# Graph tensor product: the second part's first sorting pass starts ten units into the main phase instead of beside the first sorted segment

## The chip, the cores and the metric

The kernel runs on one core of a Trainium2 chip. The core has five engines that run their own instruction streams in order: PE (TensorE: matrix products; its weight loads, PEld, overlap them), DVE (VectorE), ACT (ScalarE), POOL (GpSimd; here it issues the indirect DMAs, one row of DRAM for each of 128 partitions) and SP (SyncE; here it issues the plain DMAs). The metric is the device time of one execution in microseconds (us), the median of three runs.

## The reference, cut to what matters

```python
N, deg, C, L, DE = 10000, 64, 64, 1, 4          # E = 640000 edges, M = 4
R   = silu(edge_feat @ w_rad)                    # (E, 64)
xs  = x[src]                                     # (E, 64, 4): one 1 KB row of x for each edge
tp  = einsum('eci,ef,ifo->eco', xs, Y, cg)       # (E, 64, 4)
msg = R[:, :, None] * tp
agg = segment_sum(msg.reshape(E, 256), dst, N)   # random, unsorted destinations
out = einsum('ncm,cd->ndm', agg.reshape(N, 64, 4), w_mix)
```

Sources and destinations of the edges are drawn at random. So each edge needs a gathered row of x, and its message has to be added into a row that nothing orders.

## The kernel before

The kernel sorts the edges by destination and then sums them with matrix products. The 640,000 edges are 5,000 tiles of 128, cut into three parts (30%, 35.5% and 34.5%). Each part goes through two sorting passes:

- `pass1(k)` reads part k and writes each edge's record (9 words: source and destination packed, four Y, four features) into one of 18 groups of 576 nodes (tensor `grp`).
- `pass2` takes the groups of a part one after the other (a **segment** is one group of one part, 54 in all; the last group, which is the smallest, comes first) and writes its records into buckets of 32 nodes (tensor `bkt`). A segment's finished buckets are loaded back as `pay` (L818).

Both passes consist of a **front**, which counts digits and builds tables (`digits`, `tables`: a chain of many small operations that goes back and forth between DVE, PE and ACT, L333 to L510), and a **route**, which moves a chunk of tiles (12 in pass 1, 11 in pass 2) at a time: `spread` (L571, L574: the records spread by slot into `X`, on DVE), `rows` (L590 on DVE, L596 and L597 on ACT: one-hot matrices `oh`), `move` (L604, and in pass 2 L606 with the row carried over from the chunk before: matrix products, PE), `evict` (L611, ACT) and `store` (L615: indirect DMA from POOL). In shapes, a pass 1 chunk is 128x1512 in L574, a pass 2 chunk 128x1485 (945 for a short last one). Pass 1 works in batches of chunks, each with its own front; the first batch of a part in this phase has 14 chunks, the next ones some 12 to 13. A part of 148 chunks (the second) is counted by the planner as 878.7 steps.

`messages()` consumes the buckets. A **unit** is one bucket of one part: 313 units of 5 tiles for the first part, 313 of 6 tiles for the second and the third, 939 in all. For each unit `index` (L863 to L867, DVE) takes the sources out of `pay`, `gather` (L911, POOL) issues one indirect DMA for each tile into `xg` (7 units of buffers), PE and ACT compute the radial weights (L929 to L945), DVE multiplies them in (`products`, L963, once for each unit, which makes it the clock of this phase in the trace), and PE adds up the bucket (`sums`, L976). The buffer `xg` of a unit comes free when its `sums` are done. `messages` yields four times for each unit; such a step is called a quarter here, numbered v. A unit's index is issued 8 units, its gather 5 units ahead, so quarters 0 to 31 issue only preparations, the first unit's multiplication L963 stands at v = 30, and unit n's at about v = 30 + 4n.

The program has three stretches. First, `pass1(0)` alone. Then the **opening**: `pass2` sorts the first segment, and the loop at L1077 takes one step of `pass1(1)` after each of its steps. Then the **main phase**: a loop over v that interleaves three streams by hand, since PE, DVE and ACT are scheduled manually there (the order of the code is the order on these engines; POOL and SP are placed by the framework). For each v it first takes steps of the next part's pass 1, then steps of `pass2` for the segment that is needed next, then one quarter of `messages`. Pass 1 of the second part must end before quarter 1128, and its pace is linear:

```python
first, at, end, n = later[0]
while done < n * (v + 1 - at) / (end - at) or due:
    said = next(first, "end")
    done += said or 1
```

In the kernel before, `at` is 0, `done` starts with what the opening took (68 steps) and another 11 steps are taken in quarters 0 to 9 because `due` is set while pass 1 holds a shared PSUM bank. These 79 steps are ahead of the line that starts at 0 with a slope of 878.7/1128 = 0.779 steps a quarter, so none is taken from quarter 10 to quarter 100. The second segment has to be sorted by quarter 4 (`ends[0]`), so its sort is taken as one burst at the beginning of the main phase; from then on segments are spread over the quarters. While pass 1 holds the bank, the burst gets "held" and waits; it comes in quarter 9.

Of the kernel before, what the change touches and what calls it, by code (L numbers as in the profile page):

```python
# [68 lines left out]
def run(gen):  # L69
    for _ in gen:  # L70
        pass


class Kernel:
# [983 lines left out]
    def groups(self):  # L1058

        self.pay = {}  # L1060
        sort, main, segs, NG = self.pass2(), self.messages(), self.segs, self.NG

        ends, u = [], 0
        for k, g in segs:
            u += self.nb(g) * len(SPLIT[k][1])
            ends.append(4 * max(u - LI - 3, ends[-1] // 4 + 1 if ends else 1))

        for k in range(1, len(SPLIT)):
            ends[k * NG - 1] -= 22

        later, at = [], 0
        for k in range(1, len(SPLIT)):
            end = max(ends[k * NG - 2] - 8, at + 1)
            n = self.chunks(k)
            later.append((self.pass1(k, self.p1.NC), at, end, HEAVY * n + 20 * (n / (self.p1.NC - 2) + 2)))
            at = end
        done = 0.0  # L1077
        while segs[0] not in self.pay:
            next(sort)
            if later:  # L1080
                said = next(later[0][0])
                done += 0.0 if said == "held" else said or 1
        acc = 0.0
        i = start = 0
        for v in range(4 * u):

            if later:
                first, at, end, n = later[0]
                due = "grp" in (self.held, self.pos)
                while done < n * (v + 1 - at) / (end - at) or due:  # L1090
                    due = False
                    said = next(first, "end")
                    if said == "end":
                        later.pop(0)
                        done, self.sorted = 0.0, self.sorted + 1
                    if said in ("held", "end"):
                        break
                    done += said or 1
            if i + 1 < len(segs):
                acc += self.pass2_steps(*segs[i + 1]) / (ends[i] - start)  # L1100
                due = "bkt" in (self.held, self.pos)
                while (acc > 0.0 or v >= ends[i] or due) and segs[i + 1] not in self.pay:
                    due = False
                    said = next(sort)
                    if said == "held":
                        break
                    acc -= said or 1
                if v >= ends[i] and segs[i + 1] in self.pay:
                    i, start, acc = i + 1, ends[i], 0.0
            next(main)  # L1110
        assert not later
        run(main)
        run(sort)
# [176 lines left out]
```

## Time and profile before

| | |
|---|---|
| median of three runs | 8613.98 us (8609.68 to 8615.34) |
| the profiled execution | 8636.13 us, span 8634.0 us |
| granted TensorE clock, mean | 0.904 |
| instructions | 150016 |
| pass 1 of the first part ends | at about 527 us |
| first load of the opening (L762) | 532.6 us |
| first gather (L911) | 633.6 us |
| first unit's multiplication (L963) | 716.1 us |

The page gives busy times by engine; a table of busy times in chosen stretches shows which engine is full where, a list of instructions in order of time shows single waits ("[0.98 <-ACT pre L945]": the engine was idle for 0.98 us before this one, until ACT's L945 released it), and a group row gives count, busy time, mean duration in ns and the idle time before the group. Times count from the start of the span. The work that the change moves all lies between 532 us and the multiplication of unit 258 (2775.6 us).

### The profile page before, as it was taken

How to read it: one execution, taken by the hardware profiler on the slowest of the kernel's cores; microseconds unless marked ns; L12 is line 12 of the kernel's file. 1: busy time of each engine (PE TensorE's matmuls, PEld its weight loads, DVE VectorE, ACT ScalarE, POOL GpSimd, SP SyncE). 2: the span in 40 equal slices, each digit the busy share in tenths (PEclk: the TensorE clock that was granted, in tenths of full speed). 3: DMA queues.
4: the chain of work that ended last, by engine and by line, in shares of the span. 5: the costliest groups of instructions: out<-in, count | busy, mean ns of one | idle time of the engine just before them, and what ended most of it. 6: DMA issues, size and time to landing. Idle time of an engine off the chain costs nothing. (4 is left out here: it accounts for less than half of the span.)

```text
span 8634.0 us, 150016 instructions
## 1 busy us (share of the span) xinstructions
PE 6890.9 (80%) x52148; PEld 6320.9 (73%) x52148; DVE 6821.4 (79%) x13093; ACT 4619.2 (54%) x13164; POOL 6034.7 (70%) x6308
## 2 busy tenths in 40 slices
PE   7977888888888778888788888876888878788875
PEld 5867777777777677777777777766777767777764
DVE  7988888888888788898888988876766767676743
ACT  6867666666666465555555655534443434343421
POOL 1226777767777767777777777777777777777775
PEclk9989999999999889999999999988988989898987
DMA  9313444344434434444444444444444444444442
GB/s 160 109 58 101 121 118 119 108 115 117 122 111 116 122 104 134 134 132 138 133 132 137 133 133 133 130 139 130 128 125 125 126 124 124 122 129 124 125 123 83
DMA packets 696294, 1056.68 MB, mean 122 GB/s; under 512 B 252018, under 2 KB 500226, under 8 KB 695536
## 3 DMA queue, kind: packets, MB, share of 16 engines
q0 software_dynamic: 286560, 746.71, 30.3%
q1 hardware_dynamic: 406384, 292.76, 12.6%
q8 instruction: 412, 6.75, 0.3%
q10 hardware_dynamic: 2592, 7.63, 0.3%
q14 instruction: 346, 2.83, 0.1%
HBM read 856.08 MB, written 207.12 MB: 123 GB/s over the span
## 5 line engine op out<-in xcount | busy, mean ns | idle before, releaser
L911 POOL DMA_INDIRECT xg<-in_x_dram,sidx x5321 | 5062.5, 951 | 1713.8 <-issue 1399.6
L604 PE MATMUL pr<-X,oh 128*128 128x126 f32 (+1 forms) x21112 | 2803.6, 291 | 490.1 <-ACT rt L611 321.7
L604 PEld LDWEIGHTS pr<-X,oh 128*128 128x128 f32 x21112 | 2664.2, 202 | 584.8 <-ACT rt L611 377.8
L976 PE MATMUL G<-S,xg 128*128 128x128 f32 x21284 | 2863.7, 296 | 139.0 <-DVE Gp L1005 98.5
L976 PEld LDWEIGHTS G<-S,xg 128*128 128x128 f32 x21284 | 2715.3, 209 | 178.3 <-DVE Gp L1005 120.0
L963 DVE TENSOR_TENSOR xg<-xg,pre 128x1536 f32<-128x1536 f32 (+1 forms) x939 | 1557.8, 1659 | 888.5 <-DMA xg<-in_x_dram,sidx 648.5
L596 ACT ACTIVATE sq<-i,rowf 128x128 f32<-128x128 f32 x6403 | 1969.4, 393 | 21.7 <-DVE rowf L561 21.2
L574 DVE TENSOR_TENSOR X<-dv,Wt 128x1512 f32<-128x1512 f32 (+4 forms) x958 | 1588.4, 1658 | 221.7 <-PE pr L604 171.1
L945 ACT ACTIVATE pre<-pre 128x384 f32<-128x384 f32 (+1 forms) x939 | 431.6, 460 | 1477.3 <-PE pre L942 1125.0
L597 ACT ACTIVATE oh<-sq,ones 128x1024 f32<-128x1024 f32 (+4 forms) x958 | 1017.6, 1062 | 27.4 <-ACT sq L596 0.3
L956 DVE TENSOR_TENSOR S<-dv,pay 128x768 f32<-128x768 f32 (+1 forms) x939 | 857.4, 913 | 60.4 <-PE G L976 15.6
L615 POOL DMA_INDIRECT grp<-rt,idx x417 | 415.3, 996 | 592.5 <-ACT rt L611 256.1
L615 POOL DMA_INDIRECT bkt<-rt,idx x541 | 542.1, 1002 | 219.8 <-issue 129.2
L590 DVE TENSOR_TENSOR oh<-dv,rowf 128x512 f32<-128x512 f32 (+2 forms) x904 | 684.0, 761 | 0.5
L929 PE MATMUL pre<-identb,e 128*108 128x128 bf16 x1878 | 275.2, 230 | 418.4 <-DVE xg L963 410.9
L929 PEld LDWEIGHTS <-e 128*108 128x108 bf16 x1878 | 218.3, 133 | 496.9 <-issue 411.0
L934 ACT ACTIVATE sT<-pre 108x256 bf16<-108x256 f32 x939 | 352.3, 375 | 429.4 <-PE pre L929 428.2
L1024 PE MATMUL po<-wf,Gs 128*128 128x256 f32 (+2 forms) x1392 | 392.7, 445 | 163.6 <-DVE Gs L1005 163.3
L1024 PEld LDWEIGHTS po<-wf,Gs 128*128 128x128 f32 (+2 forms) x1392 | 284.2, 210 | 254.8 <-DVE Gs L1005 179.4
L611 ACT ACTIVATE rt<-pr 128x135 f32<-128x135 f32 (+1 forms) x958 | 258.6, 273 | 259.5 <-DMA bkt<-rt,idx 188.4
L941 PE MATMUL pre<-wr,sT 108*128 108x192 bf16 x939 | 239.7, 255 | 182.4 <-ACT sT L934 180.6
L544 ACT ACTIVATE pc<-pp 128x432 f32<-128x432 f32 (+3 forms) x506 | 243.3, 481 | 251.0 <-DVE pos L553 149.5
(240 smaller groups left out, 5347.5 us busy)
## 6 DMA issues: line engine op xcount, KB each, us to landing
xg<-in_x_dram,sidx POOLq DMA_INDIRECT x5321
sums<-Gp SPq DMA_DIRECT2D x626, 128.0 KB
old<-sums SPq DMA_DIRECT2D x626, 128.0 KB
bkt<-z SPq DMA_DIRECT2D x24, 994.5 KB
pay<-bkt SPq DMA_DIRECT2D x34, 486.0 KB
ys<-in_Y_dram SPq DMA_DIRECT2D x104, 96.0 KB
es<-in_edge_feat_dram SPq DMA_DIRECT2D x104, 96.0 KB
out_dram<-ot SPq DMA_DIRECT2D x69, 128.0 KB
```

Source lines behind the costliest of these rows:

```text
L574: nc.vector.tensor_tensor(X[:, :m, :].rearrange("p t (s w) -> p t s w", w=W), msk.unsqueeze(3).to_broadcast([P, m, ps.r, W]), QD[c // Q][1 ...
L590: nc.vector.tensor_tensor(oh[:, :v, :], self.v128.unsqueeze(1).to_broadcast([P, v, P]), row[:, o:o + v].unsqueeze(2).to_broadcast([P, v, P ...
L596: nc.scalar.activation(sq[:, u, :], self.i128, AF.Square, bias=to, scale=-1.0)
L597: nc.scalar.activation(oh[:, v:v + len(at), :], sq[:, :len(at), :], AF.Relu, bias=self.ones[:, 0:1], scale=-2.0)
L604: nc.tensor.matmul(pr[:, :ps.rw], oh[:, u, :], X[:, u, :], start=(u == 0), stop=(not on and u == m - 1))
L615: st = nc.gpsimd.indirect_dma_start(out=ps.dst, out_offset=bass.IndirectOffsetOnAxis(ap=idx[:, i:i + 1], axis=0), in_=RT.pop(c), in_offset ...
L911: nc.gpsimd.indirect_dma_start(out=xg[:, t, :], out_offset=None, in_=self.x, in_offset=bass.IndirectOffsetOnAxis(ap=si[:, u:u + 1], axis=0))
L929: nc.tensor.matmul(pre[:KR, 256 + 128 * h:384 + 128 * h], e[:, 36 * t:36 * t + KR], self.identb, start=True, stop=True)
L956: nc.vector.tensor_tensor(S[:, :ut], self.eq[:, :ut].unsqueeze(3).to_broadcast([P, ut, NB, 4]), pb[:, :, 1:5].unsqueeze(2).to_broadcast([P ...
L963: nc.vector.tensor_tensor(V, V, R.unsqueeze(3).to_broadcast([P, ut, 64, 4]), op=OP.mult)
L976: nc.tensor.matmul(G[:, h].rearrange("p n f -> p (n f)"), V[:, t, 32 * h:32 * h + 32, :].rearrange("p c i -> p (c i)"), S[:, t].rearrange( ...
L1024: nc.tensor.matmul(po[:nn, :256], Gs[:, h, f].rearrange("p b n -> p (b n)")[:, :nn], self.wf[:, h, f, :], start=(h + f == 0), stop=(h + f ...
```

## The change

The loop that sorts the first segment no longer takes a step of `pass1(1)` after each step, and the line by which `pass1(1)` is paced in the main phase starts at quarter 40 (ten units) instead of 0, with `done` = 0. Its end, quarter 1128, stays, so the slope is 878.7/1088 = 0.808 steps a quarter.

```diff
-        later, at = [], 0
+        later, at = [], 40
         for k in range(1, len(SPLIT)):
             end = max(ends[k * NG - 2] - 8, at + 1)
...
         done = 0.0
         while segs[0] not in self.pay:
             next(sort)
-            if later:
-                said = next(later[0][0])
-                done += 0.0 if said == "held" else said or 1
```

On DVE, at the beginning of the opening, the rows of the two passes alternated. Before (`dg_6054`, `two` from it and L375 with `onbkt` belong to the first segment's front, `key` and `da` to that of pass 1 of the second part):

```order
933 L772 TENSOR_SCALAR base<-bb 128x18
934 L778 TENSOR_SCALAR dg_6054<-Wt_6050 128x40
935 L779 TENSOR_SCALAR dg_6054<-dg_6054 128x40
936 L666 MEMSET k_238 1x18
937 L333 CAST two<-dg_6054 128x80
938 L690 TENSOR_SCALAR key<-da 128x168
```

and now:

```order
933 L772 TENSOR_SCALAR base<-bb 128x18
934 L778 TENSOR_SCALAR dg_6054<-Wt_6050 128x40
935 L779 TENSOR_SCALAR dg_6054<-dg_6054 128x40
936 L333 CAST two<-dg_6054 128x80
937 L338 TENSOR_TENSOR D_6057<-dv,two 128x720
938 L375 SCALAR_TENSOR_TENSOR sums<-onbkt,colsbkt 64x216
```

From row 933 to the first unit's multiplication, DVE has 425 rows before (the multiplication is row 1358) and 303 now (row 1236). Gone from there are two fronts and nine chunks of pass 1; one more chunk of the third segment now stands ahead.

On POOL, around the first gathers, the stores of pass 1 (`grp`) and pass 2 (`bkt`) and the gathers (`xg`). Before:

```order
20 L615 DMA grp<-rt,idx 165888x126 x126
21 L615 DMA bkt<-rt,idx 229888x135
22 L615 DMA grp<-rt,idx 165888x126 x2
23 L615 DMA bkt<-rt,idx 229888x135 x3
24 L911 DMA xg<-in_x_dram,sidx 128x256 x35
25 L615 DMA bkt<-rt,idx 229888x135 x12
26 L911 DMA xg<-in_x_dram,sidx 128x256 x5
```

and now:

```order
20 L615 DMA grp<-rt,idx 165888x126 x124
21 L615 DMA bkt<-rt,idx 229888x135 x4
22 L911 DMA xg<-in_x_dram,sidx 128x256 x9
23 L615 DMA bkt<-rt,idx 229888x135
24 L911 DMA xg<-in_x_dram,sidx 128x256 x7
25 L615 DMA bkt<-rt,idx 229888x135
26 L911 DMA xg<-in_x_dram,sidx 128x256 x9
27 L615 DMA bkt<-rt,idx 229888x135
28 L911 DMA xg<-in_x_dram,sidx 128x256 x10
29 L615 DMA bkt<-rt,idx 229888x135 x10
```

Four stores of pass 1 that stood ahead of the first gather now stand behind it (128 before, 124 now); the first seven units' 35 gathers stand ahead of most of the second segment's stores in both.

On DVE, just ahead of the fourth unit's multiplication L963, pass 1's first front now begins (rows L666 to L333, and L338 with `D_7490`; `Wt_6443` is the third segment's):

```order
1274 L574 TENSOR_TENSOR X<-dv,Wt_6443 128x1485
1275 L666 MEMSET k_238 1x18
1276 L690 TENSOR_SCALAR key<-da 128x168
1277 L691 TENSOR_TENSOR si<-key,si 128x168
1278 L692 TENSOR_SCALAR da<-da 128x168
1279 L333 CAST two<-da 128x336
1280 L590 TENSOR_TENSOR oh<-dv,rowf 128x512
1281 L953 TENSOR_TENSOR dv<-dv,dlc 128x160
1282 L956 TENSOR_TENSOR S<-dv,pay 128x640
1283 L338 TENSOR_TENSOR D_7490<-dv,two 128x720
1284 L963 TENSOR_TENSOR xg<-xg,pre 128x1280
```

where before (at the fifth unit's multiplication; `Wt_6939` is again the third segment's) no row of pass 1 stood for 17 units:

```order
1407 L902 TENSOR_TENSOR er<-pay,e_7990 128x100
1408 L571 TENSOR_TENSOR dv<-dv,slot 128x165
1409 L574 TENSOR_TENSOR X<-dv,Wt_6939 128x1485
1410 L953 TENSOR_TENSOR dv<-dv,dlc 128x160
1411 L956 TENSOR_TENSOR S<-dv,pay 128x640
1412 L590 TENSOR_TENSOR oh<-dv,rowf 128x512
1413 L963 TENSOR_TENSOR xg<-xg,pre 128x1280
```

Pass 1 of the second part ends at quarter 1072 before and at quarter 1074 now. From the multiplication of unit 258 to the end of the program, DVE's rows are the same ones in the same order.

## The prediction

> **What bounds the kernel now.** I read the table of busy times by stretch first, because the page's shares average over stages with different limits.
>
> ```profile
> core 0: us, PE busy (x) PEld busy (x) DVE busy (x) ACT busy (x) POOL busy (x), PEclk, DMA share, GB/s
> 536.00:716.00 180.00, 115.98 (x723) 98.31 (x724) 140.77 (x428) 105.08 (x305) 51.24 (x54) 0.76 0.18 50
> 716.00:827.00 111.00, 93.85 (x780) 87.24 (x779) 99.39 (x203) 72.84 (x212) 79.34 (x83) 0.98 0.42 120
> 827.00:2776.00 1949.00, 1619.17 (x12771) 1507.19 (x12772) 1673.70 (x3221) 1275.56 (x3716) 1418.79 (x1473) 0.92 0.41 116
> 3500.00:8500.00 5000.00, 3992.57 (x29761) 3662.86 (x29761) 3790.45 (x6853) 2340.53 (x6503) 3791.02 (x3964) 0.90 0.45 129
> ```
>
> From 3500 us to the end POOL makes 3964 indirect DMAs in 5000 us, one in 1.261 us. Next, its rows in order of time, to see what it waits for between two.
>
> ```profile
> 633.64 0.99 POOL L911 DMA_INDIRECT xg<-in_x_dram,sidx  x1 [9.55 <-DVE didx L865]
> 634.93 0.97 POOL L911 DMA_INDIRECT xg<-in_x_dram,sidx  x1 [0.30 <-issue]
> 636.21 0.95 POOL L911 DMA_INDIRECT xg<-in_x_dram,sidx  x1 [0.31 <-issue]
> ```
>
> A busy 0.95 to 0.97 us and 0.30 us of "issue" make about 1.25 us: back to back, POOL can go no faster, so from 3500 us on POOL is full although its busy share there is only 76%. Between 827 and 2776 us it makes 1473, which would need 1473 x 1.261 = 1857 of the 1949 us: 92 us short of full. There something else sets the pace at times. The multiplications L963 against their gathers tell which:
>
> ```profile
> 716.14 1.48 DVE L963 TENSOR_TENSOR xg<-xg,pre 128x1280 f32<-128x1280 f32 x1
> 826.82 1.48 DVE L963 TENSOR_TENSOR xg<-xg,pre 128x1280 f32<-128x1280 f32 x1
> 2775.64 1.49 DVE L963 TENSOR_TENSOR xg<-xg,pre 128x1280 f32<-128x1280 f32 x1 [0.98 <-ACT pre L945]
> 2834.56 1.48 DVE L963 TENSOR_TENSOR xg<-xg,pre 128x1280 f32<-128x1280 f32 x1
> ```
>
> These are units 0, 18, 258 and 270. The POOL rows that end the gathers of 258 and 270:
>
> ```profile
> 2736.14 0.95 POOL L911 DMA_INDIRECT xg<-in_x_dram,sidx  x1 [0.31 <-issue]
> 2827.74 0.94 POOL L911 DMA_INDIRECT xg<-in_x_dram,sidx  x1 [0.30 <-issue]
> ```
>
> Unit 258 is multiplied 38.6 us after its last gather was issued, unit 270 only 5.9 us after. So up to 258 the computing engines are behind and POOL waits for free buffers; then, with pass 1 of the second part over, they catch up with POOL. The waits of 716 to 2776 us agree:
>
> ```profile
> POOL xg L911 <- PE G L976: 48.9, 31, 6.0
> DVE xg L963 <- DMA xg<-in_x_dram,sidx: 13.8, 9, 4.3
> ```
>
> POOL waited 48.9 us for finished sums, DVE only 13.8 us for gathers. DVE is the fullest of the engines: 99.39 of 111 us, then 1673.70 of 1949 (86%, the rest being round trips with PE and ACT). So up to unit 258 time goes by DVE's rows, and what counts is how far unit 258 shifts: behind it DVE's rows are the same before and after.
>
> **The change, part by part.** I priced every row of DVE's order at the busy time that its line adds on the average in this trace. For the 425 rows ahead of the first multiplication that gives 140.8 us, which is the 140.77 of the first stretch; for the 303 rows now it gives 99.2 us, so 41.6 us leave the opening. The largest groups of pass 1 in the opening (536 to 716 us):
>
> ```profile
> L574 DVE TENSOR_TENSOR X<-dv,Wt 128x1512 f32<-128x1512 f32 x9 | 15.6, 1732 | 1.9 <-PE pr L604 1.4
> L590 DVE TENSOR_TENSOR oh<-dv,rowf 128x640 f32<-128x640 f32 x8 | 6.5, 815 | 0.0
> L553 DVE TENSOR_REDUCE pos<-pc 128x24 f32<-128x432 f32 x6 | 3.6, 594 | 0.4 <-ACT pc L544 0.4
> L571 DVE TENSOR_TENSOR dv<-dv,slot 128x168 f32<-128x168 f32 x9 | 3.0, 332 | 0.0
> ```
>
> Those are 28.7 us; two fronts of many small rows and less of the same kind make the rest, and a chunk and some table rows of the third segment, which now stand ahead of the first multiplication, take about 15 us back.
>
> Opening: DVE idled 180 - 140.8 = 39.2 us in it. Part of that was pass 1's doing, because DVE waited for PE behind the other pass's products:
>
> ```profile
> 578.02 1.71 DVE L574 TENSOR_TENSOR X<-dv,Wt 128x1485 f32<-128x1485 f32 x1 [3.67 <-PE pr L604]
> 591.94 1.71 DVE L574 TENSOR_TENSOR X<-dv,Wt 128x1485 f32<-128x1485 f32 x1 [4.02 <-PE pr L604]
> 618.66 0.39 DVE L465 SCALAR_TENSOR_TENSOR to<-sts,pid,gop 128x171 f32<-128x171 f32 x1 [4.00 <-PE gop L462]
> 693.10 0.24 DVE L778 TENSOR_SCALAR dg<-Wt 128x95 int32<-128x95 int32 x1 [5.25 <-DMA Wt<-grp]
> ```
>
> The first three go (11.7 us), the fourth, a load, stays. That bounds the idle time from below at 27; from above at 39, since a table chain that pass 1's rows used to fill is now bare. I take 30, nearer to the low end, because the second segment's chunks alone kept DVE nearly full. First multiplication: 536 + 99.2 + 30 = 665, 51 us earlier (42 to 54). POOL allows it: by the same prices 40.0 us of DVE's rows stand ahead of the first index where 72.4 did, so the first gather comes at about 536 + 40 + 17 = 593 instead of 633.64, and 35 gathers and nine stores (44 x 1.261 = 55) end at 649. Pass 1's loads of Y, features and indices leave SP's queue there and return ten units later; nothing in the opening waits for SP but the segments' own loads.
>
> Units 0 to 18: nothing of pass 1 stood there; now 49 steps do (60.5 quarters by 0.808). DVE's rows grow from 106.6 to 134.7 us. The stretch took 110.7 us for 106.6, so it was DVE alone; scaled alike, 134.7 take 139.9: +29. Bounds: +28 with no waits, and 134.7 / 0.859 - 110.7 = +46 with the waits of the next stretch. PE stays behind DVE: it was busy for 93.85 us of this stretch, and six chunks at 2.81 us (the row is quoted below) and small products add some 20 in 140.
>
> Units 18 to 258: the steeper line (0.808 against 0.779) adds the remaining 30 steps; DVE's rows grow by 13.1 us. At 86% that is +15, at the lowest 0, if they fall into the round trips' gaps. I take +13, since fronts and chunks come in bursts in which DVE has no gaps.
>
> POOL has four more stores behind the first gather, 4 x 1.261 = 5 us; they are covered as long as DVE leads, and the cover holds: POOL waits 48.9 us for sums. From unit 258 on everything is as before, only shifted; POOL, at most seven units ahead, shifts along.
>
> Sum: -51 + 29 + 13 = -9 us. The profiled execution took 8636.13 us, which makes 8627; it lies 22 us above the median of the runs, 8613.98, which makes **8605 us**, 0.1% less. Lowest: -54 + 28 + 0 = -26; highest: -42 + 46 + 15 = +19. About 0.2% (17 us) is what a measurement of this kernel can tell from no change, so this is a forecast of no change: work moves from one stretch where DVE sets the pace to another.
>
> **The rivals.** *POOL is the bound all along* (faster). For it: POOL is within 92 us of full already between 827 and 2776 us, and it starts 40 us earlier. Then moved DVE work would hide behind the gathers, and only the start and four stores count: -40 + 5 = -35, 8579 us. Against it: 38.6 us of backlog at unit 258, and 48.9 us of POOL waiting for sums. It decides if DVE's extra 41 us find gaps; there are 1949 - 1673.7 = 275 us of gaps, but in short round trips.
>
> *The opening runs at half clock* (slower). With fewer products PE may not earn its full clock there.
>
> ```profile
> 532.00:624.00 92.00, 54.98 (x321) 45.61 (x322) 65.69 (x204) 49.64 (x148) 7.68 (x8) 0.67 0.12 32
> 644.00:693.00 49.00, 36.80 (x262) 32.23 (x261) 39.32 (x98) 36.14 (x101) 33.21 (x35) 0.92 0.33 96
> 538.46 0.78 PE L365 MATMUL cnt<-D,sel 128*64 128x198 bf16 x4 [11.57 <-DMA es<-in_edge_feat_dram]
> 652.94 5.32 PE L604 MATMUL pr<-X,oh 128*128 128x135 f32 x22 [2.77 <-DVE oh L590]
> 660.03 2.81 PE L604 MATMUL pr<-X,oh 128*128 128x135 f32 x22 [0.56 <-ACT rt L611]
> 664.68 2.79 PE L604 MATMUL pr<-X,oh 128*128 128x135 f32 x22 [1.60 <-DVE dl L430]
> 662.69 0.39 PE L606 MATMUL pr<-rt,oh 128*128 128x135 f32 x2
> ```
>
> Even with pass 1 the granted clock was 0.67 from 532 to 624 us, and a chunk of pass 2 takes 5.32 us at the low clock instead of 2.81. Each chunk's product with the carried row waits for the eviction of the one before, so at the low clock a chunk would need 5.32 + 2 x 0.39 + about 0.3 = 6.4 us instead of the 4.65 between 660.03 and 664.68: 1.8 us more. Ahead of the first multiplication now stand 4 + 9 + 5 = 18 chunks; if all ran so, the time would be -9 + 18 x 1.8 = +23, 8637 us. It passes +17 from some 15 chunks on. Against it: with pass 2 alone, from 644 to 693 us, the clock was 0.92.
>
> [...]
>
> *The change does not do what it says.* The order rules this out for the opening; that pass 1 ends at quarter 1074 against 1072 rules out a later next part.
>
> **How the numbers follow.** The sum: 0.49, all of it counted within 0.2%. POOL, with the cases in which DVE finds gaps for most of what is moved: 0.25, faster. The clock, or waits in units 0 to 18 at their upper bound: 0.26, slower. The range reaches from the POOL case's near side (8584) to the clock's full price (8637), which leaves out about 2 in 10.
>
> **What would show it.** First gather near 593, first multiplication near 665 (654 to 674), unit 18 near 805, unit 258 near 2767, and from there the same shift to the end. DVE nearly full in units 0 to 18, POOL's waits for sums longer there. Wrong in the first term if the first multiplication is later than 680; wrong in the second if units 0 to 18 take under 125 or over 157 us; wrong altogether if unit 258 shifts otherwise than the end does.

## The result and the profile after

The changed kernel takes 8595.4 us (median of 18 runs, 8588.25 to 8604.24); the kernel before, run beside it, takes 8611.53 us (18 runs, 8601.73 to 8620.35). The ratio is 0.9982, with a 95% interval of 0.9974 to 0.9989: 16 us less, a gain that is real and lies just inside the 0.2% that the prediction called no change. The forecast was 8605.

The profiled execution of the changed kernel took 8589.39 us (span 8587.6). In it the opening begins at 515.4 us instead of 532.6. That difference of 17 us lies ahead of every changed instruction: among the six profiled executions of these kernels on such chips the opening began between 515.4 and 537.8 us, the changed kernel itself at 535.3 in another one. So in what follows, times count from the first load of the opening (L762) of the same execution.

The table of busy times by stretch, changed kernel (columns as in the prediction's first fence; the first four stretches are the opening and units 0 to 18, 18 to 90 and 90 to 258):

```profile
core 0: us, PE busy (x) PEld busy (x) DVE busy (x) ACT busy (x) POOL busy (x), PEclk, DMA share, GB/s
519.00:646.00 127.00, 79.20 (x511) 66.03 (x511) 95.83 (x299) 77.39 (x218) 49.41 (x52) 0.77 0.21 57
646.00:782.00 136.00, 115.27 (x919) 106.68 (x919) 128.96 (x279) 90.28 (x267) 96.12 (x101) 0.94 0.42 121
782.00:1364.00 582.00, 480.67 (x3794) 446.11 (x3793) 505.99 (x1003) 377.26 (x1101) 421.48 (x439) 0.92 0.40 116
1364.00:2730.00 1366.00, 1134.96 (x9019) 1058.61 (x9020) 1183.15 (x2268) 904.96 (x2636) 979.18 (x1018) 0.93 0.40 114
3500.00:8500.00 5000.00, 3978.04 (x29745) 3653.18 (x29743) 3773.85 (x6807) 2327.03 (x6461) 3791.91 (x3965) 0.90 0.45 130
```

The prediction took units 18 to 258 of the kernel before in one piece (827 to 2776 us). Cut at unit 90, the same view of the kernel before reads:

```profile
core 0: us, PE busy (x) PEld busy (x) DVE busy (x) ACT busy (x) POOL busy (x), PEclk, DMA share, GB/s
827.00:1422.00 595.00, 490.42 (x3840) 454.86 (x3841) 505.46 (x981) 383.82 (x1119) 440.04 (x457) 0.91 0.41 117
1422.00:2776.00 1354.00, 1128.75 (x8933) 1052.33 (x8933) 1168.24 (x2242) 891.74 (x2599) 978.76 (x1016) 0.93 0.40 115
```

The reader is to see two things. Units 18 to 90 became 13 us shorter although DVE is as busy there as before (505.99 against 505.46 us); POOL has 18 DMAs less to make there, 439 against 457, and 101 instead of 83 in units 0 to 18. Units 90 to 258 became 12 us longer, with 15 us more of DVE's rows.

The first two gathers, and the multiplications of units 0, 18, 90 and 258 (POOL's and DVE's rows in order of time, changed kernel):

```profile
567.44 0.99 POOL L911 DMA_INDIRECT xg<-in_x_dram,sidx  x1 [10.34 <-DVE didx L865]
568.73 0.97 POOL L911 DMA_INDIRECT xg<-in_x_dram,sidx  x1 [0.30 <-issue]
...
645.49 1.49 DVE L963 TENSOR_TENSOR xg<-xg,pre 128x1280 f32<-128x1280 f32 x1
781.56 1.48 DVE L963 TENSOR_TENSOR xg<-xg,pre 128x1280 f32<-128x1280 f32 x1
1363.44 1.48 DVE L963 TENSOR_TENSOR xg<-xg,pre 128x1280 f32<-128x1280 f32 x1
2729.59 1.48 DVE L963 TENSOR_TENSOR xg<-xg,pre 128x1280 f32<-128x1280 f32 x1
```

From these rows come the stretches (before, unit 90 is multiplied at 1421.93 us); the column f1 is another profiled execution of the changed kernel, on another chip (run f1 below).

| stretch | before | changed | difference | changed, f1 | predicted difference |
|---|---|---|---|---|---|
| opening to first multiplication | 183.5 | 130.1 | -53.4 | 131.5 | -51 |
| units 0 to 18 | 110.7 | 136.1 | +25.4 | 135.1 | +29 |
| units 18 to 90 | 595.1 | 581.9 | -13.2 | 583.2 | |
| units 90 to 258 | 1353.7 | 1366.2 | +12.5 | 1365.8 | |
| units 18 to 258 together | 1948.8 | 1948.1 | -0.7 | 1949.0 | +13 |
| opening to unit 258 | 2243.0 | 2214.2 | -28.8 | 2215.6 | -9 |
| opening to the last multiplication | 8020.0 | 7992.6 | -27.4 | 7998.6 | same shift as 258 |

In the traces the gain up to unit 258 is 27 to 29 us, and 21 to 27 of it reaches the last multiplication; the medians show 16. A trace is a single execution, and where the remaining 5 to 11 us go is not known. So two of the three terms hold and the third, units 18 to 258, is where the forecast was about 14 us too high.

The waits between 646 and 2730 us, the same stretch of work as 716 to 2776 us before (us in total, times, longest):

```profile
POOL xg L911 <- PE G L976: 69.7, 30, 9.7
DVE xg L963 <- DMA xg<-in_x_dram,sidx: 13.7, 7, 4.0
```

POOL starts earlier and has to wait more for finished sums, 69.7 against 48.9 us; DVE waits for gathers as little as before.

### The profile page after: what moved, and what is told of

It is laid out like the page before. It is cut to its first block, busy times and chain, and to the rows that moved or that the text cites. A ratio compares the mean times of both kernels' runs of the same rounds, so it can differ in the third digit from the quotient of the medians.

```text
span 8587.6 us, 149978 instructions
## 1 busy us (share of the span) xinstructions
PE 6864.6 (80%) x52148; PEld 6301.3 (73%) x52148; DVE 6822.0 (79%) x13093; ACT 4618.6 (54%) x13164; POOL 6032.2 (70%) x6308
## 5 line engine op out<-in xcount | busy, mean ns | idle before, releaser
L963 DVE TENSOR_TENSOR xg<-xg,pre 128x1536 f32<-128x1536 f32 (+1 forms) x939 | 1558.1, 1659 | 878.3 <-DMA xg<-in_x_dram,sidx 663.3
L574 DVE TENSOR_TENSOR X<-dv,Wt 128x1512 f32<-128x1512 f32 (+4 forms) x958 | 1588.6, 1658 | 223.6 <-PE pr L604 172.3
L945 ACT ACTIVATE pre<-pre 128x384 f32<-128x384 f32 (+1 forms) x939 | 430.9, 459 | 1482.9 <-PE pre L942 1156.6
L544 ACT ACTIVATE pc<-pp 128x396 f32<-128x396 f32 (+3 forms) x506 | 242.8, 480 | 251.3 <-DVE pos L553 156.7
```

The source lines that it names most:

```text
L574: nc.vector.tensor_tensor(X[:, :m, :].rearrange("p t (s w) -> p t s w", w=W), msk.unsqueeze(3).to_broadcast([P, m, ps.r, W]), QD[c // Q][1 ...
L963: nc.vector.tensor_tensor(V, V, R.unsqueeze(3).to_broadcast([P, ut, 64, 4]), op=OP.mult)
```

## The experiments

Two theories were put first. **A**: every microsecond of DVE's rows up to unit 258 costs its own length, wherever it stands. **B**: work in units 18 to 258 falls into DVE's gaps and is free, while work ahead of unit 18 costs its length. The runs named e and g came to two other chips, on which the kernel before takes some 10,490 us at a granted clock of 0.84; their ratios are to the kernel before on the same chip. The runs named f were made on a chip like the first (kernel before: 8630.04 us).

### On a chip like the first

**f1**, the changed kernel again.

> The changed kernel itself, beside the next three on the same chip, as their reference. Ratio to the kernel before 0.998 (0.997 to 0.999). In its profile: opening 130 us, units 0 to 18 136 us, units 18 to 258 1948 us where the chip runs like the one of the first profiles; where it runs like the one of the four runs before (10490 us), about 150, 180 and 2430 us.

Measured: 8612.07 us, 0.9980 of the kernel before (0.9971 to 0.9989). The gain repeats, and so do the stretches (table above).

**f2**, the changed kernel with the start at quarter 100 instead of 40.

```diff
-        later, at = [], 40
+        later, at = [], 100
```

> Start at quarter 100, nothing in the opening, once more, now beside the changed kernel. Against the changed kernel 32 us of DVE's rows move from units 0 to 18 to units 18 to 258. Theory A (all of DVE's rows up to unit 258 cost their length): same time as the changed kernel within 5 us. Theory B (units 0 to 18 have no gaps on DVE, units 18 to 258 have): 25 us less than the changed kernel in units 0 to 18, at most 10 us more behind, ratio to before 0.995 to 0.9965.

Measured: 8638.80 us, 1.0011 (1.0002 to 1.0020), a little slower than the kernel before and 27 us slower than the changed one. Theory A had it level with the changed kernel and theory B ahead of it; both are wrong here. Busy times by stretch (units 0 to 18, 18 to 90, 90 to 258; columns as above):

```profile
669.00:779.00 110.00, 90.75 (x731) 85.28 (x730) 96.03 (x198) 64.75 (x188) 76.55 (x80) 0.92 0.43 122
779.00:1373.00 594.00, 489.33 (x3805) 454.22 (x3805) 512.67 (x1024) 375.71 (x1102) 432.88 (x451) 0.91 0.41 117
1373.00:2779.00 1406.00, 1168.47 (x9207) 1090.17 (x9206) 1205.12 (x2326) 929.18 (x2710) 988.08 (x1026) 0.92 0.39 112
```

The opening keeps its gain (131.2 us) and units 0 to 18 are as short as before (110). But units 90 to 258 take 52 us more than before, for 37 us more of DVE's rows and 40 us more of PE's. Steps that go behind unit 90 cost more than their length on DVE.

**f3**, the changed kernel with a useless copy of 128x256 on DVE behind L574 in each chunk of the second part's pass 1.

```diff
+            if ps is self.p1 and ps.NC == 14 and self.sorted == 1:
+                nc.vector.tensor_copy(self.pad[:, :256], self.pad[:, :256])
...
+        self.pad = self.ph.tile([P, 256], F, name="pad", bufs=1)
+        self.nc.vector.memset(self.pad, 0.0)
```

> The changed kernel with one more DVE copy (128x256, in place, of no use) after each chunk of pass 1 of the second part, 148 of them, most of them between units 18 and 258. At 0.25 to 0.35 us each they are 37 to 52 us of DVE's time. Theory A: units 18 to 258 take 37 to 60 us longer, the whole 1.004 to 1.007 of the changed kernel. Theory B: under a third of it, 0 to 15 us, 1.000 to 1.002 of the changed kernel.

Measured: 8625.57 us, 0.9995 (0.9986 to 1.0004), 13.5 us more than the changed kernel. All 148 copies are there, 141 of them between units 18 and 258 (group row of that stretch):

```profile
L580 DVE COPY pad<-pad 128x256 f32<-128x256 f32 x141 | 43.8, 310 | 0.0
```

These 43.8 us of DVE's time, with 2 us more ahead of unit 18, cost 13.5, or about 0.3 us for 1. By theory A they cost their length, and that falls; two thirds went into DVE's gaps, as B says. So a busy DVE is not what a step costs. A step also brings products for PE, evictions for ACT and the chain of waits between them, and f2 shows that whole steps behind unit 90 do not fit into the gaps.

**f4**, the kernel before, with its overlap in the opening kept, and only the line started at quarter 40.

```diff
-        later, at = [], 0
+        later, at = [], 40
```

> Half of the change: the opening still takes a step of pass 1 after each of its steps, but the line that paces pass 1 in the main phase starts at quarter 40. The 79 steps of the opening are now ahead of that line until quarter 137 instead of 101. Both theories: opening and units 0 to 18 as before, units 18 to 258 within 5 us, ratio to before 0.9995 to 1.001. If the steeper line costs or gains anything by itself, it shows here.

Measured: 8651.04 us, 1.0025 (1.0016 to 1.0034): 21 us slower, where both theories had it level. The trace has 6 of these 21 us by unit 258 and 12 by the last multiplication; the rest is not located. By the mean prices of the lines, DVE's rows up to unit 258 are the same 1977.3 us in sum; what moves is about 15 us of them from units 18 to 90 to units 90 to 258:

```profile
823.00:1417.00 594.00, 471.93 (x3729) 438.99 (x3727) 491.13 (x955) 371.68 (x1081) 437.03 (x455) 0.91 0.41 116
1417.00:2780.00 1363.00, 1130.11 (x9017) 1053.66 (x9017) 1183.85 (x2268) 906.43 (x2639) 979.39 (x1018) 0.93 0.40 115
```

Taking 14 us of DVE's rows and 18 us of PE's out of units 18 to 90 left that stretch as long as it was (594 against 595), while the same rows behind unit 90 added 9 us. What was lost in units 18 to 90, when units 0 to 18 are short, lies at their beginning. Units 18 to 28 of the kernel before, then of the changed one:

```profile
827.00:910.00 83.00, 65.31 (x524) 61.72 (x525) 61.09 (x93) 50.92 (x148) 59.80 (x63) 0.90 0.41 116
```

```profile
782.00:846.00 64.00, 52.76 (x434) 49.00 (x433) 54.85 (x108) 36.66 (x108) 48.46 (x52) 0.95 0.46 131
```

These ten units are 19 us shorter now, for 7 us less of DVE's rows; units 28 to 90 take 518 us instead of 512, with 7 us more of them. When unit 18 was multiplied, its last gather had been issued 16 us before, in the changed kernel 45 us before. In the kernel before POOL works without a pause from 755 to 882 us, 101 DMAs in 127 us, and is late all the same. DVE did not have to wait for gathers there. What came too late were POOL's stores. SP's load of a segment's records (L762) waited 29.0 us for a store of pass 1. SP's queue issued nothing between 853.4 us and that load at 882.51 us, and the stores of finished sums (L1009), which stand behind the load there, followed from 883.90 us on; ACT's L1007, which writes the buffer `Gp` that they read, stopped for 12.36 us until one had landed, and DVE stopped for 9.56 us for the load (rows of the kernel before, in order of time):

```profile
880.17 1.01 POOL L615 DMA_INDIRECT grp<-rt,idx  x1 [0.30 <-issue]
882.51 0.33 SPq L762 DMA_DIRECT2D Wt<-grp  x1
886.22 0.24 DVE L778 TENSOR_SCALAR dg<-Wt 128x95 int32<-128x95 int32 x1 [9.56 <-DMA Wt<-grp]
887.22 0.38 ACT L1007 ACTIVATE Gp<-G 128x256 f32<-128x256 f32 x1 [12.36 <-DMA sums<-Gp]
```

The waits of this kind in units 18 to 90, first of the kernel before (827 to 1422 us), then of f4 (823 to 1417), then of the changed kernel (782 to 1364), where ACT and DVE have none:

```profile
SPq L762 <- DMA grp<-rt,idx: 49.8, 3, 29.0
SPq L818 <- DMA bkt<-rt,idx: 14.3, 4, 8.3
ACT Gp L1007 <- DMA sums<-Gp: 21.7, 3, 12.4
DVE dg L778 <- DMA Wt<-grp: 11.1, 2, 9.6
```

```profile
SPq L818 <- DMA bkt<-rt,idx: 50.0, 4, 28.3
SPq L762 <- DMA grp<-rt,idx: 43.3, 3, 18.8
ACT Gp L1007 <- DMA sums<-Gp: 35.5, 4, 24.8
```

```profile
SPq L818 <- DMA bkt<-rt,idx: 8.7, 3, 3.5
SPq L762 <- DMA grp<-rt,idx: 0.7, 1, 0.7
```

SP waits 64 us for POOL's stores in the kernel before, 93 in f4, 25 in f2, but 9 in the changed kernel and 7 in f1; ACT's waits behind them are 21.7, 35.5, 13.0 and twice nothing. The three with such waits take 594 or 595 us, whatever DVE has to do (491 to 513 us), the two without 582 and 583. In f4, where DVE has less to do there, the gathers of units 25 to 27 came late too: DVE stood idle for 22.5 us ahead of their multiplications, and the last 9 of these went to ACT's stop of 24.8 us. The changed kernel makes 18 more of POOL's DMAs in units 0 to 18, which take 25 us longer, so POOL is not late behind them.

From these runs came a third theory, put more widely than the waits bear out. **C**: between units 18 and 90 POOL sets the pace, so steps in units 0 to 90 are cheap while POOL uses the time to get ahead; behind unit 90 steps cost about their length (f4: 9 us for 16 of DVE's rows; the changed kernel: 12.5 for 15; f2: 52 for 37).

### On the slower chips

**e0**, the kernel before itself, as a measure of the comparison.

> The kernel before, unchanged, as a control. In its first profiled execution the first load of the opening came at 532.6 us, in the changed kernel's at 515.4 us, although no instruction of the stretch ahead of it is changed. If that difference of 17 us is chance, this profile's opening may begin anywhere between the two, the opening (from that load to the first multiplication) takes 183 us again, units 0 to 18 take 111 us and units 18 to 258 take 1949 us, each within 5 us. The ratio to the kernel before is 1.000 within 0.001.

Measured: 10489.78 us, 1.0005 (0.9996 to 1.0015). The same program waits for other things there. Busy times from 3500 to 8500 us, and some of the largest waits of PE, DVE and ACT over the whole span ("remote": no event on this core shows what released the engine):

```profile
3500.00:8500.00 5000.00, 3626.24 (x24633) 3284.24 (x24634) 3278.23 (x6138) 2095.74 (x5911) 3020.03 (x3157) 0.83 0.37 104
```

```profile
PE G L976 <- issue: 481.4, 598, 11.6
PE pr L604 <- issue: 367.8, 482, 10.3
DVE Gs L1005 <- remote: 722.0, 136, 16.1
ACT pre L945 <- remote: 1128.0, 194, 18.6
```

POOL makes 3157 DMAs in 5000 us where it made 3964 on the first chip: it is not full there, and PE, DVE and ACT stand still, up to 18.6 us at a time, without an instruction of this core that the trace names as what they wait for. What is cheap and what is dear there says little about the first chip.

**e1**, the changed kernel with the start at quarter 0, and **e3**, with the start at quarter 100 (the edit of f2).

```diff
-        later, at = [], 40
+        later, at = [], 0
```

> Pass 1 of the second part starts with quarter 0, nothing of it in the opening. By DVE's order, priced as in the prediction, 110 us of its rows stand ahead of the first multiplication (99 in the changed kernel, 141 before), 139 us in units 0 to 18 (135, 107), and nothing is added in units 18 to 258. Theory A (every us of DVE's rows up to unit 258 costs about its own length): opening 141 us, units 0 to 18 about 141, units 18 to 258 1949: 12 us less than before, about the same as the changed kernel. Theory B (work that is added to units 18 to 258 costs nothing because DVE has gaps there, work ahead of unit 18 costs its own length): also 12 us less than before, but about 16 us more than the changed kernel, ratio 0.9985 to 0.999.

> Pass 1 of the second part starts with quarter 100 (after unit 17), nothing of it in the opening. The opening is that of the changed kernel (130 us, 53 less than before), units 0 to 18 hold DVE's rows of the kernel before (about 107 to 111 us), and units 18 to 258 get 44 us more of them. Theory A: -53 - 3 + 44 to 51, between -12 and -5 us against before, ratio 0.9986 to 0.9994. Theory B: the 44 us fall mostly into gaps (0 to 12 us longer), -56 to -44 us, ratio 0.9935 to 0.995. The rival that POOL sets the pace all along expects the same as B at its far end, 0.9935.

Measured: e1 10464.37 us, 0.9981 (0.9971 to 0.9990); e3 10431.27 us, 0.9950 (0.9935 to 0.9965). On that chip the later start is the better one. In e3 units 90 to 258 take 1706.8 us against 1719.7 in e0, with 39 us more of DVE's rows (1207.1 against 1168.1): there such work was free, as theory B says. On a chip like the first, f2 showed the opposite.

**e4**, in the opening 20 steps of pass 1 (its first front) and no more, the rest from quarter 40.

```diff
             next(sort)
+            if later and (done < 20 or "grp" in (self.held, self.pos)):
+                said = next(later[0][0])
+                done += 0.0 if said == "held" else said or 1
```

> The opening takes only the first front of pass 1 (20 steps, until it lets go of the shared bank), no chunk; the rest starts with quarter 40. DVE's rows: 109 us ahead of the first multiplication (99 in the changed kernel), 123 in units 0 to 18 (135), as in the changed kernel behind. If the front fills waits of the first segment's table chain, the opening stays near 130 us and units 0 to 18 take 125 instead of 136: 11 us less than the changed kernel, ratio to before 0.9965 to 0.9975. If it delays the chain by its own length, the opening takes 140 us and the time is that of the changed kernel, 0.998.

Measured: 10475.93 us, 0.9990 (0.9981 to 0.9999). The opening takes 157.0 us against 214.4 in e0, nearly all that the removal gives there, and units 0 to 18 get 14 us longer; units 18 to 258 take 20 us more. Its ratio is no better than that of the plain change on the other slower chip (g4, 0.9961).

The last four were meant to test theory C on a chip like the first, and came to slower ones. **g1** and **g2** bend the line of the changed kernel: by quarter 390 (unit 90) pass 1 is 50, or 100, steps further, and it ends where it did.

```diff
-                while done < n * (v + 1 - at) / (end - at) or due:
+                more = 50 * min((v + 1 - at) / 350, (end - v - 1) / (end - at - 350)) if at == 40 else 0.0
+                while done < n * (v + 1 - at) / (end - at) + more or due:
```

**g3** is e1 again, **g4** the changed kernel.

> The changed kernel with a bent line: the second part's pass 1 still starts at quarter 40 and still ends near quarter 1128, but by quarter 390 (unit 90) it is 50 steps further than the straight line. By the mean prices of the lines, 35.7 us of DVE's rows move from units 90-258 to units 0-90, and eight stores of POOL with them. Theory A (every us of DVE's rows up to unit 258 costs its own length): the same as the changed kernel, 0.998 of the kernel before (0.997 to 0.999). Theory B (work put into units 18-258 is free, work ahead of unit 18 costs its length): 3 us more than the changed kernel, 0.9984. Theory C (POOL sets the pace between units 18 and 90, DVE behind unit 90): units 0-90 grow by 10 to 20 us from 718, units 90-258 shrink by 29 to 50 us from 1366; in sum 15 to 30 us faster than the changed kernel, 0.9945 to 0.9965.

> The same bend, 100 steps: 64.5 us of DVE's rows and some 17 stores move from units 90-258 to units 0-90. Theory A: the same as the changed kernel, 0.998. Theory B: 8 us more than the changed kernel, 0.999. Theory C: units 90-258 shrink by 52 to 90 us; DVE's rows in units 0-90 are then 721 us, more than POOL's 560 rows there need, so that DVE sets the pace there too, and units 0-90 grow by 35 to 60 us; in sum 5 to 35 us faster than the changed kernel, 0.994 to 0.9975, and no more than twice the gain of the bend of 50 steps.

> The overlap in the opening removed as in the changed kernel, but pass 1 of the second part starts at quarter 0 of the main phase. Against the kernel before, DVE's rows: opening -32.5 us, units 0-90 +34.6, units 90-258 -2.1. Theory A: only idle time of the opening is saved, 9 us, 0.999. Theory C: opening -40 us, units 0-90 +15 to +25, units 90-258 -2: 17 to 27 us faster, 0.997 to 0.998, that is as fast as the changed kernel or up to 10 us faster.

> The changed kernel beside the three others on one chip: 0.998 of the kernel before (0.997 to 0.999), opening 131 us, units 0-18 135 us, units 18-90 582 us, units 90-258 1366 us.

Measured, beside 10487.8 us of the kernel before: g1 10442.89 us, 0.9961 (0.9947 to 0.9974); g2 10459.59, 0.9978 (0.9967 to 0.9989); g3 10457.75, 0.9971 (0.9959 to 0.9983); g4 10445.93, 0.9961 (0.9948 to 0.9975). Units 18 to 90 and 90 to 258, first g4, then g1:

```profile
846.00:1567.00 721.00, 540.29 (x3797) 492.11 (x3795) 504.56 (x1003) 378.25 (x1103) 420.08 (x437) 0.85 0.33 93
1567.00:3285.00 1718.00, 1278.89 (x9016) 1167.25 (x9017) 1184.22 (x2268) 907.87 (x2637) 982.29 (x1020) 0.85 0.32 91
```

```profile
859.00:1640.00 781.00, 587.23 (x4072) 532.64 (x4070) 539.11 (x1068) 412.01 (x1203) 431.04 (x448) 0.84 0.31 88
1640.00:3310.00 1670.00, 1232.41 (x8801) 1128.58 (x8802) 1146.52 (x2198) 874.60 (x2541) 975.64 (x1015) 0.86 0.33 93
```

There the bend adds 60 us to units 18 to 90 and saves 48 behind them, for 35 and 38 us of DVE's rows: a step costs 1.3 to 1.7 times its DVE rows on either side, and g1 gains nothing over g4. C's gain of 15 to 30 us did not come. Since POOL is not full on these chips (437 DMAs in 721 us; SP waited for POOL's stores for 2 us in g4 and 16 in e0 between units 18 and 90), C's condition is not met there, and g1 and g2 neither prove nor refute it for the first chip. g3 came within the range that C gave, with A's 0.999 outside its interval, but for the same reason that is no support. The stretches expected of g4 were those of the first chip, so they did not come either.

The changed kernel gains more on the slower chip, 0.4%. Its opening takes 148.4 us there against the 214.4 of e0 on the other slower chip, a gain of 66, of which units 0 to 18 take back 11 and the later stretches some more.

No kernel here beats the changed one on a chip like the first. On the slower ones the start at quarter 100 has the lowest ratio, 0.9950.

## Why the prediction was right, and where it was not

**The opening, -51: right.** Measured -53.4 and, in f1, -52.0. Counted from 519 us, as the prediction counted from 536, DVE was busy for 95.83 us (predicted 99.2) and idle for 31 (predicted 30, bounds 27 and 39). The first gather came 49 us earlier, where 40 were predicted: between the first load and it DVE was busy for 39 us, about as priced, and idle for 13, not the 20 that were put in (17 from 536 us on). That moved nothing else, since the first multiplication waits for DVE's rows.

**Units 0 to 18, +29: nearly right.** Measured +25.4 and +24.4, a little under the lower bound of 28. The prices are 6 to 7 us too high on both sides (106.6 and 134.7 us, where the profile has 99.39 and 128.96), so the stretch before was not DVE alone: it had 11.6 us of idle time, of which 7.0 are left. DVE's busy time grew by 29.6 us, as priced, and the idle time shrank by 4.6.

**Units 18 to 258, +13: mis-sized.** Measured -0.7 and, in f1, +0.2. The step that failed is "at 86% that is +15, at the lowest 0 ... I take +13", which treats 240 units as one stretch with one price. It is two. Behind unit 90 the price was about right: 15 us more of DVE's rows cost 12.5 us. But the kernel before had lost time just behind unit 18 that the prediction did not see: units 0 to 18 without pass 1 ran so fast through the gathers made in advance that POOL fell behind, and its late stores stopped SP, and through SP ACT and DVE. The prediction had the sign of this at hand, POOL 92 us short of full on the average of 1949 us, and spread it evenly; in units 18 to 28 its 63 DMAs need 79 of 83 us. It took the four added stores of POOL as covered "as long as DVE leads", and the way from a late store over SP's queue is not in it. The change spreads DVE's work from units 0 on, POOL is ahead at unit 18, and 13 us return between units 18 and 90. With the third term at 0 the sum would have been -22.

That POOL's lateness is the cause rests on the waits and counts in the traces of five runs and on f4's stretch that did not get shorter with less work in it. No run moves these stores or loads alone. The experiment made to prove theory C (g1, g2) came to chips where it could not show, so the price of a step ahead of unit 90 on the first chip is known only from the runs that are here.

**The cover of POOL's four stores: right for the changed kernel.** POOL's waits for sums grew from 48.9 to 69.7 us, as was said they would. It was the kernel before in which POOL's stores were not covered.

**The same shift to the end: right within some us.** -28.8 at unit 258, -27.4 at the last multiplication; -27.4 and -21.4 in f1. The forecast of the time came closer than its working: by the traces the shift of -9 missed by 12 to 18 us, by the medians by 7. That closeness is luck.

**The rivals.** *POOL is the bound all along* would be -35; the traces show -21 to -27 at the end, nearer to it than to the sum, and the medians -16, nearer to the sum. But its reason fails as it was put: were POOL the bound all along, f2 would have gained as much as the changed kernel, and it lost. Something of it holds just behind unit 18 of the kernel before. *The opening runs at half clock* fell. PE's rows in the opening of the changed kernel, in order of time:

```profile
539.42 5.22 PE L604 MATMUL pr<-X,oh 128*128 128x135 f32 x22 [2.91 <-DVE oh L590]
544.98 2.82 PE L604 MATMUL pr<-X,oh 128*128 128x135 f32 x22
...
567.10 5.17 PE L604 MATMUL pr<-X,oh 128*128 128x135 f32 x22 [1.50 <-DVE oh L590]
573.15 2.82 PE L604 MATMUL pr<-X,oh 128*128 128x135 f32 x22
...
624.05 5.72 PE L604 MATMUL pr<-X,oh 128*128 128x135 f32 x22 [1.68 <-DVE oh L590]
630.66 2.82 PE L604 MATMUL pr<-X,oh 128*128 128x135 f32 x22
```

Only the first chunk behind each front ran at the low clock, three in all: it took 5.17 to 5.72 us at a granted clock of 0.50 to 0.55, and the second 2.82 us at 1.00. The granted clock from 519 to 646 us is 0.77 (0.73 in f1), against 0.76 before. *The change does not do what it says* fell with the opening.

## What to carry to other kernels

A stretch in which one engine runs ahead uses up the lead of the engine that feeds it (here POOL's, 16 us at unit 18 against 45 in the changed kernel), and the bill comes in the next stretch. Here it came not by the gathers but by stores that the same engine made too late, on which a load waits in another queue, with all that stands behind it. So before pricing moved work, cut the profile where the lead is gone, compare for each piece the feeding engine's count times its pitch with the piece's length, and read the waits of the DMA queue itself. A busy share averaged over 1949 us had hidden a piece of 83 us in which POOL was full and late. And a step is more than its rows on the fullest engine: added DVE time alone cost about 0.3 us for 1 us here, whole steps behind unit 90 0.6 to 1.4 us for 1 us of their DVE rows.

## What was not expected of the hardware

The same program took 8611 to 8630 us on some chips and 10,488 to 10,490 us on two others, at a granted clock of 0.90 and 0.84. The clock is not all of it: PE's busy time grew from 6890.9 to 7630.1 us, and the span by 1856. Much of the rest is idle time for which the trace names no instruction of this core: in the kernel before none of the waits reads "remote" on the first chip, and on the slower one ACT's wait at L945 alone sums to 1128.0 us so. These stops are not scattered by chance: most recur at the same rows of the program. ACT's 7331st row (with its waits counted as rows), in order of time, first in e0, then the corresponding row in g1, which ran on the other of the two chips, then the same row of the kernel before on the first chip:

```profile
4172.01 0.47 ACT L945 ACTIVATE pre<-pre 128x384 f32<-128x384 f32 x1 [13.80 <-remote]
```

```profile
4152.77 0.47 ACT L945 ACTIVATE pre<-pre 128x384 f32<-128x384 f32 x1 [13.85 <-remote]
```

```profile
3452.86 0.48 ACT L945 ACTIVATE pre<-pre 128x384 f32<-128x384 f32 x1 [2.93 <-DVE Gp L1005]
```

In e1 and g3, the same program on the two slower chips, ACT has 181 waits of over 6 us in e1 that read "remote"; 152 of them read so again, over 3 us long, at the same row in g3. So most of them belong to a place in the instruction streams, and chips of the first kind do not show them; what makes an engine stop there stays open. It also means that a change worth 0.2% on one chip can be worth 0.4%, or have the other sign, on another: the start at quarter 100 was 1.0011 and 0.9950.
